# Layer two's unit in a two-layer MLP after attention: seven products in one row, twelve triples in another, its chains queued behind copies, its weights' conversions spread

## The chip, the cores and the metric

The kernel runs on one core of one Trainium2 chip. The metric is the device time of one execution in microseconds; the median of three runs stands for a kernel. One more execution was recorded by the hardware profiler, and all rows below are from that one.

Five engines work side by side, each with its own queue in order: TensorE (PE; its weight loads are listed as PEld), VectorE (DVE), ScalarE (ACT), GpSimd (POOL) and SyncE (SP), which issues the DMAs here. An instruction that has to wait for another engine or a DMA waits at the head of its queue, and all behind it wait too.

## The reference

```python
def _attn_ref(q, k, v):                      # B, H, S, D = 4, 8, 576, 64
    scores = scale * np.matmul(q, k.transpose(0, 1, 3, 2))
    # heads 0-3: mask rel in [0, 32);  heads 4-7: rel >= 0 and same position mod 32
    attn = softmax(np.where(masks, scores, -1e9))
    return np.matmul(attn, v)
x = attn_out.transpose(0, 2, 1, 3).reshape(2304, 512)
# layer one: w_in [512, 2048], w_out [2048, 512]
h = x @ w_in;  g = s * np.maximum(h, 0) ** 2 + b;  x = g @ w_out
# layer two: same shapes
h = x @ w_in;  g = h * np.cos(h);  out = g @ w_out
```

The weights come as 8-byte floats and are converted on the chip. Every operand of a large matmul is split into a high and a low part (two tensors in the matmul's reduced 4-byte format), and each product of matrices is made of three matmuls: high by high, low by high, high by low.

## The kernel before

**Stages.** Attention runs first and overlaps the beginning of layer one. Layer one goes over the 2048 hidden features in four passes (`NPASS`) of 20 slots (`PER`): a slot `t` is one of five blocks of tokens (512 four times, then 256) by one of four groups of 128 features. In a slot `mm_h` makes h in 12 matmuls (4 input chunks, 3 each), `run_act` spreads Relu, Square (ACT), scale and shift (DVE), the high part (ACT) and the low part (DVE) over the ticks that follow, and `mm_2` adds the slot before last into four accumulators in PSUM (12 matmuls). At the end of a block `run_evac` adds the four accumulators to the tile `part` in SBUF: the DVE line L724.

**Background work in layer one.** `bg_step` takes operations of a list that converts the layer's own next weights (`wraw`, `wtmp`); `bg2_step` does the same for layer two's weights, to be stored in DRAM in the form that layer two reads (`wf`, `w2s`). There are 32 such jobs: 16 of `pair_ops` (17 steps each: `praw` loaded, `ta`, `ts`, `ob`, `oa`) and 16 of `out_ops` (9 steps: `oraw`, `tw`, `ow`). The first step of each is an ACT operation (L135) on the raw data that a DMA has landed. `BG2 = 0.85` steps are due after each eighth of a slot from the second pass on; steps left over are done before layer two.

**Layer two** takes three thirds of the tokens (768 each, `SBT`) by eight pairs of feature groups: 24 units `u`. A unit makes h for two groups of 128 features and two halves of 384 tokens by seven products instead of eight (Strassen's scheme with sums shared, on operands that `run_forms` prepares in seven slots of `xhi` and `xlo`). A product is six matmuls of 384 columns into one of two PSUM banks (`pa`, `pb`; they change roles from unit to unit). Copies of a bank to SBUF (`q`, ACT, L1076) and sums of a bank and a copy (`hsum`, DVE, L1049) give the two h of a unit, f = 0 and 1. `run_act2` then makes h·cos(h) of each h: two ACT operations that reduce the argument (`r` L966 and `a` L967), one on DVE (L969), Sin on ACT (L971), the product with h on DVE (L973), high part on ACT and low part on DVE. Six **triples** for each f (three matmuls of 512 columns, `acc`, L1016) add it to six accumulators, which are the output.

**What sets the order.** The code records operations in the order of the list `UNIT`: a product's name, or `t` for one triple. After each entry `beat` advances every generator in `stages` by one step, which places the steps of `run_act2` and `run_forms` between products and triples. A triple is taken from `queue` only if its g was recorded at least `READY_AFTER = 6` beats ago. A scheduler then turns the record into one order for each engine, and moves an operation forward where it reckons the engine idle and the operation ready. `PRODUCTS` gives for each product its weights, its slot of x, its bank, and whether it starts a new sum in the bank or adds to what is there (P6, P7 and P3 add). A product that starts anew, or adds after a copy, may begin only when the copy or sum that reads its bank has ended.

Of the kernel before, what the change touches and what calls it, by code (L numbers as in the profile page):

```python
# [1 line left out]

# [72 lines left out]
    "P1": (0, 0, 0, 0, True),  # L75
    "P5": (1, 0, 1, 1, True),
    "P6": (1, 1, 2, 0, False),
    "P7": (2, 0, 3, 0, False),
    "P2": (0, 1, 5, 0, True),
    "P3": (2, 1, 6, 1, False),  # L80
    "P4": (3, 0, 4, 0, True),
}
LAST_USE = {"P6": 1, "P2": 0, "P3": 2, "P4": 3}
UNIT = ["P1", "t", "P5", "t", "t", "P6", "t", "t", "t", "P7", "t", "t", "t", "P2", "t", "P3", "t", "P4", "t"]
BG2 = 0.85
FORM_PACE = 4
READY_AFTER = 6
LOADS = {
# [9 lines left out]
def net(ctx, tc, qk, rqk, vloc, vstr, rv, w1, w2, s, b, out):  # L98
# [563 lines left out]
    def mm_h(t, c):  # L662
# [4 lines left out]
        for i, (wi, xt) in enumerate(((0, xhi), (0, xlo), (1, xhi))):  # L667
# [7 lines left out]
            )  # L675

    def run_act(t):
# [162 lines left out]
    def run_forms(s_):  # L840
# [30 lines left out]
        whole = (0, HT)  # L871
        yield from split(0, block(0, 0))
        t1 = temp(0)
        sub(t1, b_(0, 1), b_(0, 0), 0, 1)
        yield
        yield from split(1, [(whole, t1)])
        t2 = temp(1)
        sub(t2, b_(1, 1), t_(t1), 1)
        yield
        yield from split(2, [(whole, t2)])  # L880
        t3 = temp(0)
        sub(t3, b_(1, 1), b_(0, 1), 1)
        yield
        yield from split(3, [(whole, t3)])
        sub(t2, b_(1, 0), t_(t2), 0)
        yield
        yield from split(4, [(whole, t2)])
        yield from split(5, block(1, 0))
        yield from split(6, block(1, 1))

    def paced(gen, n):
        for _ in gen:
            for _ in range(n):
                yield

# [18 lines left out]
    for t in range(NSLOT):  # L914
# [35 lines left out]
    while jobs2 or loaded2 or now2[0]:  # L950
# [6 lines left out]
    queue = [("first", t, e) for t in (NSLOT - 2, NSLOT - 1) for e in range(NC)]  # L957
    g2, g2_at = {}, {}
    clock = [0]

    def run_act2(u, f, h, parts):
        gh = gl = None
        for a, b in parts:
# [9 lines left out]
            nc.vector.tensor_tensor(r, h[:, a:b], r, ALU.mult)  # L973
            yield
            if gh is None:
                gh = g_p.tile([P, SBT], F32R, tag="gh", name="gh2")
                gl = g_p.tile([P, SBT], F32R, tag="gl", name="gl2")
            split_hi(gh[:, a:b], r)
# [4 lines left out]
        g2_at[u, f] = clock[0]  # L983

# [9 lines left out]

    def triple(wait=False):

        if not queue:
            return False
        kind, a, *b = queue[0]
        if kind == "first":  # L1000
            queue.pop(0)
            mm_2(a, b[0])
            if b[0] == NC - 1:
                load_w2(4 + a - (NSLOT - 2))
            return True
        f, e = b
        key = a, f
        if key not in g2 or (not wait and clock[0] < g2_at[key] + READY_AFTER):
            return False
        queue.pop(0)  # L1010
        s_, p = divmod(a, NPAIR)
# [15 lines left out]
        if p == NPAIR - 1 and f == 1:  # L1027
            spawn(run_out(s_, e))
        return True

    def beat():
        clock[0] += 1
        tick()

    HALVES = [slice(0, HT), slice(HT, SBT)]
    for u in range(NSB * NPAIR):
        s_, p = divmod(u, NPAIR)
        if p == 0 and s_ + 1 < NSB:
            stages.append(paced(run_forms(s_ + 1), FORM_PACE))
        lastu = u == NSB * NPAIR - 1  # L1040
# [5 lines left out]
        def hsum(f, half, bank, q):  # L1046
            if f not in hs:
                hs[f] = h_p.tile([P, SBT], F32, tag="hs", name="h2")
            nc.vector.tensor_tensor(hs[f][:, HALVES[half]], bank, qs[q], ALU.add)  # L1049

        for what in UNIT:
            if what == "t":
                triple()
                beat()
                continue
            x, fi, j, bi, st = PRODUCTS[what]
            while (s_, j) not in formed:
                beat()
            xh, xl = x_slot(s_, j)
# [7 lines left out]
            if p == NPAIR - 1:  # L1067
                used.add((s_, j))
            if what in LAST_USE:
                i = 4 * u + LAST_USE[what]  # L1070
                del wft[i]
            beat()
            if what in ("P1", "P6", "P7"):
                q = {"P1": 0, "P6": 1, "P7": 2}[what]
                qs[q] = (rem_p, rem_p, gt_p)[q].tile([P, HT], F32, tag=("rq", "rv", "gt")[q], name="q")
                nc.scalar.activation(qs[q], pb[0], AF.Copy)  # L1076
# [10 lines left out]
            if what == "P2":  # L1087
                load_wf(4 * u + 7)
                load_wf(4 * u + 8)
            if what == "P3":  # L1090
                load_wf(4 * u + 9)
            if what == "P4":
                load_wf(4 * u + 10)
        queue.extend(("mm", u, f, e) for f in range(2) for e in range(SBT // P))
    while queue:
        triple(True)
        beat()
    while stages:
# [74 lines left out]
```

## Time and profile before

| | us |
|---|---|
| median of three runs | 884.03 |
| the three runs | 884.03, 890.0, 883.83 |
| the profiled execution | 889.94 |
| its span, first to last instruction | 888.2 |
| PE busy in the span | 869.2 |
| DVE busy | 594.4 |
| ACT busy | 515.2 |

The profiled execution is like the slowest of the three runs, 5.9 above the median. A busy PE is not one at its pace: a matmul's end is modelled, and the pace is read from one start to the next.

### The profile page before, as it was taken

The numbers are of one execution on the slowest core, as the hardware profiler recorded it, in microseconds if no ns is written. First come the engines' busy times: TensorE is split into PE (matmuls) and PEld (weight loads), VectorE is DVE, ScalarE is ACT, GpSimd is POOL, SyncE is SP. The second block draws the span as 40 slices with busy tenths as digits, with TensorE's granted clock in tenths as the row PEclk, the third lists the DMA queues.
The fourth block names the chain that finished last, engine by engine and source line by source line (L and its number), as shares of the span: only waits on it lengthen the run. The fifth ranks groups of instructions, "written<-read, shape, count | busy, mean of one in ns | idle before, by whom it ended". The sixth has DMA issues, their size and how long they took to land.

```text
span 888.2 us, 13475 instructions
## 1 busy us (share of the span) xinstructions
PE 869.2 (98%) x4901; PEld 737.8 (83%) x4901; DVE 594.4 (67%) x1265; ACT 515.2 (58%) x1123; POOL 4.0 (0%) x15
## 2 busy tenths in 40 slices
PE   8899999999999999999999989999999999999998
PEld 5577777898777887888888978989889898988986
DVE  5978889999889996343579564547745446554554
ACT  5878898667556654343466363646646355463544
POOL 1000000000000000000000000000000000000000
PEclk9989999999999999999999999999999999999999
DMA  9655442775667662012104555655665565755611
GB/s 271 186 148 163 146 144 76 270 261 175 221 249 247 222 212 74 1 48 72 47 10 180 195 174 176 202 168 187 216 212 201 167 194 180 246 198 166 205 56 72
DMA packets 65058, 147.39 MB, mean 166 GB/s; under 512 B 6256, under 2 KB 24688, under 8 KB 64992
## 3 DMA queue, kind: packets, MB, share of 16 engines
q1 hardware_dynamic: 64992, 146.53, 50.2%
q8 instruction: 39, 0.64, 0.3%
q14 instruction: 27, 0.22, 0.1%
HBM read 118.72 MB, written 27.79 MB: 165 GB/s over the span
## 4 chain that ended last, share of the span: by engine, by line
PE 76%; DVE 10%; DMA 7%; ACT 4%; issue 2%; SPq 1%; ACTq 0%; DVEq 0%
PE acc L1016 22%; PE h_ps L668 14%; PE acc L704 14%; PE pa L1064 10%; PE pb L1064 10%; DMA wraw<-in_w_dram 3%; PE o_ps L533 3%; PE s_ps L500 2%; PE t_ps L457 1%; DMA wearly<-in_w_dram 1%; DVE part L724 1%; ACT part L432 1%; DVE r L687 1%; DVE gl L130 1%; DMA praw<-in_w_dram 1%
## 5 line engine op out<-in xcount | busy, mean ns | idle before, releaser
L704 PE MATMUL acc<-gh,w 128*128 128x512 f32 (+1 forms) x640 | 198.0, 371 | 5.1 <-DVE part L724 5.0
L668 PE MATMUL h_ps<-xhi,w 128*128 128x512 f32 (+1 forms) x640 | 197.9, 372 | 1.0 <-ACT w L127 1.0
L1016 PE MATMUL acc<-w2l,gh 128*128 128x512 f32 x576 | 180.1, 393 | 0.0
L704 PEld LDWEIGHTS acc<-gh,w 128*128 128x128 f32 x640 | 117.3, 188 | 27.9 <-DVE part L724 8.1
L668 PEld LDWEIGHTS h_ps<-xhi,w 128*128 128x128 f32 x640 | 117.0, 189 | 22.0 <-ACT w L127 1.2
L668 PE MATMUL h_ps<-xlo,w 128*128 128x512 f32 (+1 forms) x320 | 119.3, 373 | 0.1
L704 PE MATMUL acc<-gl,w 128*128 128x512 f32 (+1 forms) x320 | 118.3, 370 | 0.0
L1016 PEld LDWEIGHTS acc<-w2l,gh 128*128 128x128 f32 x576 | 106.8, 189 | 11.9
L1016 PE MATMUL acc<-w2l,gl 128*128 128x512 f32 x288 | 114.2, 397 | 0.0
L966 ACT ACTIVATE r<-h 128x768 f32<-128x768 f32 (+1 forms) x50 | 41.0, 820 | 114.5 <-DVE h L1049 114.2
L127 ACT ACTIVATE gh<-r 128x512 fp32r<-128x512 f32 (+3 forms) x130 | 87.5, 675 | 34.3 <-DVE r L687 28.0
L130 DVE TENSOR_TENSOR gl<-r,gh 128x512 fp32r<-128x512 f32 (+3 forms) x130 | 96.6, 745 | 14.6 <-ACT gh L127 13.5
L1064 PE MATMUL pb<-xhi,wfl 128*128 128x384 f32 x336 | 100.7, 340 | 2.4 <-ACT q L1076 2.4
L1064 PE MATMUL pa<-xhi,wfl 128*128 128x384 f32 x336 | 99.9, 338 | 0.0
L681 ACT ACTIVATE r<-h_ps 128x512 f32<-128x512 f32 (+1 forms) x80 | 43.9, 549 | 64.0 <-PE h_ps L668 63.9
L1049 DVE TENSOR_TENSOR h<-pb,q 128x384 f32<-128x384 f32 x48 | 26.7, 557 | 74.2 <-PE pb L1064 48.5
L1049 DVE TENSOR_TENSOR h<-pa,q 128x384 f32<-128x384 f32 x48 | 26.7, 557 | 69.2 <-PE pa L1064 48.6
L668 PEld LDWEIGHTS h_ps<-xlo,w 128*128 128x128 f32 x320 | 60.5, 189 | 10.6 <-DVE xlo L130 0.4
L704 PEld LDWEIGHTS acc<-gl,w 128*128 128x128 f32 x320 | 60.3, 189 | 9.7
L1064 PEld LDWEIGHTS pb<-xhi,wfl 128*128 128x128 f32 x336 | 62.6, 189 | 6.6 <-ACT q L1076 3.0
L1064 PEld LDWEIGHTS pa<-xhi,wfl 128*128 128x128 f32 x336 | 62.2, 188 | 3.6
L687 DVE TENSOR_SCALAR r<-r,sb 128x512 f32<-128x512 f32 (+1 forms) x72 | 37.0, 513 | 42.0 <-ACT r L682 41.8
(105 smaller groups left out, 1280.0 us busy)
## 6 DMA issues: line engine op xcount, KB each, us to landing
wfl<-wf SPq DMA_DIRECT2D x72, 512.0 KB, 4.6
w2l<-w2s SPq DMA_DIRECT2D x48, 512.0 KB, 3.3
wraw<-in_w_dram SPq DMA_DIRECT2D x56, 256.0 KB, 3.2
praw<-in_w_dram SPq DMA_DIRECT2D x32, 256.0 KB, 3.4
oraw<-in_w_dram SPq DMA_DIRECT2D x16, 512.0 KB
wf<-ob SPq DMA_DIRECT2D x16, 512.0 KB, 2.7
w2s<-ow SPq DMA_DIRECT2D x16, 512.0 KB, 4.3
wfl<-wf SPq DMA_DIRECT2D x24, 256.0 KB, 2.7
```

The source lines that it names most:

```text
L127: nc.scalar.activation(dst_hi, src, AF.Copy)
L130: nc.vector.tensor_tensor(dst_lo, src, hi.bitcast(F32), ALU.subtract)
L500: it.last = nc.tensor.matmul(it.s_ps[po : po + lq.shape[1], co : co + lk.shape[1]], lq, lk, start=not pe_mask, stop=True, skip_group_check ...
L533: nc.tensor.matmul(dst, vs, pt, start=True, stop=True)
L668: nc.tensor.matmul(h_ps[t][:, :tb], wt[:, wi, c * P : (c + 1) * P], xt[:, c, t0 : t0 + tb], start=(c == 0 and i == 0), stop=(c == NC - 1 a ...
L681: nc.scalar.activation(r, h, AF.Relu)
L687: nc.vector.tensor_scalar(r, r, sb[:, 0:1], sb[:, 1:2], ALU.mult, ALU.add)
L704: nc.tensor.matmul(o, wt[:, wi, e * P : (e + 1) * P], g, start=f == 0 and i == 0, stop=f == FP - 1 and i == 2, skip_group_check=True,)
L966: nc.scalar.activation(r, h[:, a:b], AF.Copy, bias=0.25, scale=INV_2PI)
L1016: nc.tensor.matmul(accs[e], g[:, e * P : (e + 1) * P], w[:, wi, :], start=p == 0 and f == 0 and i == 0, stop=p == NPAIR - 1 and f == 1 and ...
L1049: nc.vector.tensor_tensor(hs[f][:, HALVES[half]], bank, qs[q], ALU.add)
L1064: nc.tensor.matmul(pb[bi], a, b[:, m, :], start=st and m == 0 and i == 0, stop=m == 1 and i == 2, skip_group_check=True)
```

## The change

The seven products of a unit now stand in one row and its twelve triples in another. `UNIT` is `P1 P2 P6 P5 P7`, then one `t` that stands for all twelve triples, then `P3 P4`, which the next unit's `P1` follows. The triples are those of the unit before last (`TRIPLE_LAG = 2`), with no clock of beats; in units 0 and 1 four accumulations left from layer one stand in their place (`first`), and 24 triples follow after the last unit.

P2 changes banks and sums with the copy of P1 while P6 is made. The steps of f = 0 are recorded from P3 on as before. Those of f = 1 now start only after P5 of the **next** unit, and are tied: `r` is issued behind the copy of P6 of that unit, `a` behind the copy of P7. `tc.issue_after(x)` gives no wait at run time; it holds an operation behind `x` in the order of the engine that both run on. `run_forms` moves one step after every four triples, behind the last copy and the last sum, and prepares the slots in another order.

In layer one the pace of the conversions of layer two's weights is 0.85 in the second and third pass and 1.25 in the fourth, and the first step of each job is tied behind the last Relu that was recorded. A Sin on one element is recorded in slot 64, behind a Relu, so that the ACT table with Sin is loaded there.

```diff
 PRODUCTS = {
     "P1": (0, 0, 0, 0, True),
-    "P5": (1, 0, 1, 1, True),
+    "P2": (0, 1, 1, 1, True),
     "P6": (1, 1, 2, 0, False),
...
-UNIT = ["P1", "t", "P5", "t", "t", "P6", "t", "t", "t", "P7", "t", "t", "t", "P2", "t", "P3", "t", "P4", "t"]
-BG2 = 0.85
+UNIT = ["P1", "P2", "P6", "P5", "P7", "t", "P3", "P4"]
+BG2 = (0.0, 0.85, 0.85, 1.25)
 FORM_PACE = 4
-READY_AFTER = 6
+TRIPLES = 12
+TRIPLE_LAG = 2
...
                 now2[0] = loaded2.pop(0)
                 bg2_load()
+                with tc.issue_after(relu[0].ins):
+                    next(now2[0])()
+                continue
...
-        nc.scalar.activation(r, h, AF.Relu)
+        relu[0] = nc.scalar.activation(r, h, AF.Relu)
...
+        if last == 4:
+            with tc.issue_after(relu[0].ins):
+                nc.scalar.activation(sb[:, 4:5], sb[:, 3:4], AF.Sin)
...
-                bg2_step(BG2)
+                bg2_step(BG2[t // PER])
...
+        def act(step, *args, **kw):
+            key = (after or {}).get(step)
+            with tc.issue_after(evac[key].ins) if key else nullcontext():
+                nc.scalar.activation(*args, **kw)
...
-            nc.scalar.activation(r, h[:, a:b], AF.Copy, bias=0.25, scale=INV_2PI)
-            nc.scalar.activation(m, r, AF.Copy, bias=MAGIC)
+            act("r", r, h[:, a:b], AF.Copy, bias=0.25, scale=INV_2PI)
+            while held("m"):
+                yield
+            act("m", m, r, AF.Copy, bias=MAGIC)
...
+    def form_step(u):
+        if forms and (u, 2) in evac:
+            with tc.issue_after(evac[u, 2].ins), tc.issue_after(added[u].ins):
+                if next(forms[0], "end") == "end":
+                    forms.pop(0)
+
+    def triples(u):
+        n = 0
+        while queue and (n < NC if queue[0][0] == "first" else queue[0][1] <= u - TRIPLE_LAG):
+            triple()
+            tick()
+            n += 1
+            if n % FORM_PACE == 0:
+                form_step(u)
+        for _ in range(n, TRIPLES):
+            tick()
...
+            if what == "P2":
+                hsum(0, 0, pb[1], 0)
+            if what == "P5" and u:
+                spawn(run_act2(u - 1, 1, h1.pop(), [(0, SBT)], {"r": (u, 1), "m": (u, 2)}))
             if what == "P7":
                 hsum(1, 1, pb[1], 2)
-            if what == "P2":
-                hsum(0, 0, pb[0], 0)
             if what == "P3":
                 hsum(0, 1, pb[1], 1)
                 spawn(run_act2(u, 0, hs[0], parts))
             if what == "P4":
                 hsum(1, 0, pb[0], 2)
-                spawn(run_act2(u, 1, hs[1], parts))
+                if lastu:
+                    spawn(run_act2(u, 1, hs[1], parts))
+                else:
+                    h1.append(hs[1])
```

**PE in a unit of layer two.** Before, products (`pa`, `pb`; five rows, six matmuls) and triples (`acc`; two rows) change places all along the unit:

```order
L1016 MATMUL acc_5419<-w2l,gl_6432 128x512
L1064 MATMUL pa<-xhi,wfl 128x384
L1064 MATMUL pa<-xlo,wfl 128x384
L1064 MATMUL pa<-xhi,wfl 128x384 x2
L1064 MATMUL pa<-xlo,wfl 128x384
L1064 MATMUL pa<-xhi,wfl 128x384
L1016 MATMUL acc_5420<-w2l,gh_6431 128x512 x2
L1016 MATMUL acc_5420<-w2l,gl_6432 128x512
L1016 MATMUL acc_5421<-w2l,gh_6431 128x512 x2
L1016 MATMUL acc_5421<-w2l,gl_6432 128x512
L1064 MATMUL pb<-xhi,wfl 128x384
```

Of the changed kernel, the end of a row of twelve triples and the first two products, P3 and P4, of the row of seven:

```order
L1028 MATMUL acc_5425<-w2l,gh_6579 128x512 x2
L1028 MATMUL acc_5425<-w2l,gl_6580 128x512
L1090 MATMUL pb<-xhi,wfl 128x384
L1090 MATMUL pb<-xlo,wfl 128x384
L1090 MATMUL pb<-xhi,wfl 128x384 x2
L1090 MATMUL pb<-xlo,wfl 128x384
L1090 MATMUL pb<-xhi,wfl 128x384
L1090 MATMUL pa<-xhi,wfl 128x384
L1090 MATMUL pa<-xlo,wfl 128x384
L1090 MATMUL pa<-xhi,wfl 128x384 x2
```

Seven products follow one another with no triple between them, and so do twelve triples.

**ACT in a unit of layer two.** Before, in one unit of the last third (`r` and `a` reduce the argument, the second `r<-r` line is Sin, `gh` the high part, `q` a copy):

```order
L1076 ACTIVATE q<-pb 128x384 x2
L966 ACTIVATE r_7155<-h_7139 128x768
L967 ACTIVATE a_7156<-r_7155 128x768
L966 ACTIVATE r_7173<-h_7122 128x768
L967 ACTIVATE a_7174<-r_7173 128x768
L971 ACTIVATE r_7155<-r_7155 128x768
L1076 ACTIVATE q<-pa 128x384
L971 ACTIVATE r_7173<-r_7173 128x768
L127 ACTIVATE gh_7192<-r_7155 128x768
L127 ACTIVATE gh_7209<-r_7173 128x768
L1076 ACTIVATE q<-pa 128x384 x2
```

Of the changed kernel, from f = 0 of one unit (`r_6891`) to its f = 1 (`r_6945`):

```order
L973 ACTIVATE r_6891<-h_6796 128x768
L973 ACTIVATE a_6892<-r_6891 128x768
L1099 ACTIVATE q<-pa 128x384
L988 ACTIVATE r_6891<-r_6891 128x768
L1099 ACTIVATE q<-pa 128x384
L973 ACTIVATE r_6945<-h_6831 128x768
L973 ACTIVATE gh_6933<-r_6891 128x768
L1099 ACTIVATE q<-pa 128x384
L973 ACTIVATE a_6946<-r_6945 128x768
L988 ACTIVATE r_6945<-r_6945 128x768
L129 ACTIVATE xhi<-part 128x2x384
L973 ACTIVATE gh_6981<-r_6945 128x768
```

The three copies of the next unit (P1, P6, P7) now stand one by one in the chain of f = 0, each behind one or two operations on 768 columns, and f = 1 follows them.

**ACT in layer one.** Before, a stretch of the second pass (Relu L681, Square L682, first steps of jobs `ta` and `tw`):

```order
L681 ACTIVATE r<-h_ps 128x512
L682 ACTIVATE r<-r 128x512
L135 ACTIVATE tw<-oraw 128x512
L127 ACTIVATE gh<-r 128x512
L127 ACTIVATE ob<-ts 128x4x128
L127 ACTIVATE oa<-ta 128x2x128
L127 ACTIVATE oa<-ta 128x128
L135 ACTIVATE tw<-oraw 128x512
L681 ACTIVATE r<-h_ps 128x512
```

Of the changed kernel, also in the second pass:

```order
L688 ACTIVATE r<-h_ps 128x512
L137 ACTIVATE tw<-oraw 128x512
L689 ACTIVATE r<-r 128x512
L129 ACTIVATE w_3673<-wtmp 128x512
L129 ACTIVATE gh<-r 128x512
L137 ACTIVATE wtmp<-wraw 128x256
L129 ACTIVATE ow<-tw 128x512
L137 ACTIVATE wtmp<-wraw 128x256
L688 ACTIVATE r<-h_ps 128x512
```

A job's first step now stands right behind a Relu and ahead of that slot's Square. Counted over the whole order of ACT, the 32 first steps stood 10, 16, 1 and 5 to the four passes, and stand 1, 9, 11 and 11 now.

## Rows read from the trace of the kernel before

**Rows 1.** Windows: stretch, length, busy us of PE, PEld, DVE, ACT, POOL, clock, DMA share.
```profile
206.00:304.00 98.00, 93.55 (x445) 77.41 (x444) 88.56 (x206) 60.20 (x121) 0.00 (x0) 1.00 0.67 227
304.00:402.00 98.00, 97.31 (x470) 81.68 (x469) 60.01 (x135) 45.52 (x90) 0.00 (x0) 1.00 0.30 94
499.00:884.00 385.00, 382.63 (x1896) 343.84 (x1895) 207.27 (x279) 200.69 (x295) 0.00 (x0) 1.00 0.54 179
```
**Rows 2.** Waits: who waited for whom, us in total, times, longest.
```profile
PE acc L704 <- DVE part L724: 5.0, 7, 1.6
```
**Rows 3.** Timeline, 229 to 233 us, ACT, DVE and PE: start, us, instruction [idle before].
```profile
229.92 0.43 ACT L135 ACTIVATE wtmp<-wraw 128x256 f32<-128x256 f32 x1 [2.97 <-DMA wraw<-in_w_dram]
...
230.91 0.55 DVE L687 TENSOR_SCALAR r<-r,sb 128x512 f32<-128x512 f32 x1 [2.92 <-ACT r L682]
...
230.12 0.39 PE L704 MATMUL acc<-gh,w 128*128 128x512 f32 x1
232.11 0.50 PE L704 MATMUL acc<-gh,w 128*128 128x512 f32 x1 [1.60 <-DVE part L724]
```
**Rows 4.** Windows of the tile praw alone: stretch, length, busy DVE, ACT (counts), clock, DMA.
```profile
206.00:304.00 98.00, 9.63 (x14) 5.23 (x8) 1.00 0.67 227
```
**Rows 5.** The chain that ended last, one unit of layer two: start, us, matmuls.
```profile
622.73 1.39 PE acc L1016 x6
...
627.24 1.06 PE pa L1064 x6
...
638.49 1.39 PE acc L1016 x6
```
**Rows 6.** Timeline, PE, 508 to 510 us: two products in succession.
```profile
508.13 0.33 PE L1064 MATMUL pa<-xhi,wfl 128*128 128x384 f32 x1
508.30 0.33 PE L1064 MATMUL pa<-xlo,wfl 128*128 128x384 f32 x1
...
509.17 0.33 PE L1064 MATMUL pb<-xhi,wfl 128*128 128x384 f32 x1
```
**Rows 7.** Timeline, PE, 871 to 875 us: first, fourth and fifth of the last triples.
```profile
871.31 0.63 PE L1016 MATMUL acc<-w2l,gh 128*128 128x512 f32 x2
...
873.39 0.62 PE L1016 MATMUL acc<-w2l,gh 128*128 128x512 f32 x2
...
874.07 0.62 PE L1016 MATMUL acc<-w2l,gh 128*128 128x512 f32 x2
```
**Rows 8.** Timeline, 648 to 652 us: a product's successor on PE, its sum, the chain's start.
```profile
648.82 0.63 PE L1016 MATMUL acc<-w2l,gh 128*128 128x512 f32 x2
649.02 0.56 DVE L1049 TENSOR_TENSOR h<-pa,q 128x384 f32<-128x384 f32 x1 [1.20 <-PE pa L1064]
649.67 0.85 ACT L966 ACTIVATE r<-h 128x768 f32<-128x768 f32 x1 [5.07 <-DVE h L1049]
650.55 0.85 ACT L967 ACTIVATE a<-r 128x768 f32<-128x768 f32 x1
651.37 0.85 ACT L966 ACTIVATE r<-h 128x768 f32<-128x768 f32 x1
```
**Rows 9.** Timeline, 511 to 516 us, ACT and PE: the beginning of layer two.
```profile
511.31 0.47 ACT L1076 ACTIVATE q<-pb 128x384 f32<-128x384 f32 x1
511.80 1.28 ACT L971 ACT_TABLE_LOAD   x1
...
511.83 0.44 PE L1064 MATMUL pb<-xhi,wfl 128*128 128x384 f32 x1 [0.42 <-ACT q L1076]
512.11 0.34 PE L1064 MATMUL pb<-xlo,wfl 128*128 128x384 f32 x1
...
515.10 0.52 PE L1064 MATMUL pb<-xhi,wfl 128*128 128x384 f32 x1 [1.95 <-ACT q L1076]
```
**Rows 10.** Windows: the two stretches at the lower clock, columns as in rows 1.
```profile
44.30:51.10 6.80, 6.80 (x54) 5.69 (x54) 4.80 (x14) 3.73 (x8) 0.00 (x0) 0.50 0.40 117
...
515.30:518.70 3.40, 3.40 (x10) 3.04 (x10) 3.01 (x5) 2.64 (x4) 0.00 (x0) 0.50 0.03 11
```

More of the change, by code (lines that the diff above doesn't have):

```diff
@@ L1 @@
 import math
+from contextlib import nullcontext
 import concourse.bass as bass
@@ L75 @@
     "P1": (0, 0, 0, 0, True),
-    "P5": (1, 0, 1, 1, True),
+    "P2": (0, 1, 1, 1, True),
     "P6": (1, 1, 2, 0, False),
-    "P7": (2, 0, 3, 0, False),
-    "P2": (0, 1, 5, 0, True),
+    "P5": (1, 0, 3, 1, True),
+    "P7": (2, 0, 4, 0, False),
     "P3": (2, 1, 6, 1, False),
-    "P4": (3, 0, 4, 0, True),
+    "P4": (3, 0, 5, 0, True),
 }
-LAST_USE = {"P6": 1, "P2": 0, "P3": 2, "P4": 3}
-UNIT = ["P1", "t", "P5", "t", "t", "P6", "t", "t", "t", "P7", "t", "t", "t", "P2", "t", "P3", "t", "P4", "t"]
-BG2 = 0.85
+LAST_USE = {"P2": 0, "P5": 1, "P3": 2, "P4": 3}
+UNIT = ["P1", "P2", "P6", "P5", "P7", "t", "P3", "P4"]
+BG2 = (0.0, 0.85, 0.85, 1.25)
 FORM_PACE = 4
-READY_AFTER = 6
+TRIPLES = 12
+TRIPLE_LAG = 2
 LOADS = {
@@ L675, in mm_h @@
             )
+    relu = [None]
     def run_act(t):
@@ L872, in run_forms @@
         yield from split(0, block(0, 0))
+        yield from split(1, block(1, 0))
         t1 = temp(0)
@@ L875, in run_forms @@
         yield
-        yield from split(1, [(whole, t1)])
         t2 = temp(1)
@@ L880, in run_forms @@
         yield from split(2, [(whole, t2)])
+        yield from split(3, [(whole, t1)])
         t3 = temp(0)
@@ L883, in run_forms @@
         yield
-        yield from split(3, [(whole, t3)])
+        yield from split(4, [(whole, t3)])
         sub(t2, b_(1, 0), t_(t2), 0)
         yield
-        yield from split(4, [(whole, t2)])
-        yield from split(5, block(1, 0))
+        yield from split(5, [(whole, t2)])
         yield from split(6, block(1, 1))
[L891 to L894, printed above, removed]
     wft, w2t = {}, {}
@@ L957, in net, with run_act2, held @@
     queue = [("first", t, e) for t in (NSLOT - 2, NSLOT - 1) for e in range(NC)]
-    g2, g2_at = {}, {}
-    clock = [0]
-    def run_act2(u, f, h, parts):
+    g2 = {}
+    evac, added = {}, {}
+    def run_act2(u, f, h, parts, after=None):
         gh = gl = None
+        def act(step, *args, **kw):
+            key = (after or {}).get(step)
+            with tc.issue_after(evac[key].ins) if key else nullcontext():
+                nc.scalar.activation(*args, **kw)
+        def held(step):
+            return after and step in after and after[step] not in evac
         for a, b in parts:
@@ L974, in run_act2 @@
             yield
+            while held("hi"):
+                yield
             if gh is None:
@@ L977, in run_act2 @@
                 gl = g_p.tile([P, SBT], F32R, tag="gl", name="gl2")
-            split_hi(gh[:, a:b], r)
+            act("hi", gh[:, a:b], r, AF.Copy)
             yield
@@ L982, in run_act2 @@
         g2[u, f] = (gh, gl)
-        g2_at[u, f] = clock[0]
     def run_out(s_, e):
@@ L993, in run_out, with triple @@
         nc.sync.dma_start(out=out[r0 : r0 + P, :], in_=o)
[L995 to L999, printed above, removed]
+    def triple():
+        kind, a, *b = queue.pop(0)
         if kind == "first":
-            queue.pop(0)
             mm_2(a, b[0])
@@ L1004, in triple @@
                 load_w2(4 + a - (NSLOT - 2))
-            return True
+            return
         f, e = b
         key = a, f
-        if key not in g2 or (not wait and clock[0] < g2_at[key] + READY_AFTER):
-            return False
-        queue.pop(0)
         s_, p = divmod(a, NPAIR)
@@ L1028, in triple @@
             spawn(run_out(s_, e))
[L1029 to L1033, printed above, removed]
+    forms = []
+    def form_step(u):
[13 more added lines that the diff above has]
+            tick()
     HALVES = [slice(0, HT), slice(HT, SBT)]
+    h1 = []
     for u in range(NSB * NPAIR):
@@ L1038, in net @@
         if p == 0 and s_ + 1 < NSB:
-            stages.append(paced(run_forms(s_ + 1), FORM_PACE))
+            forms.append(run_forms(s_ + 1))
         lastu = u == NSB * NPAIR - 1
@@ L1048, in hsum @@
                 hs[f] = h_p.tile([P, SBT], F32, tag="hs", name="h2")
-            nc.vector.tensor_tensor(hs[f][:, HALVES[half]], bank, qs[q], ALU.add)
+            added[u] = nc.vector.tensor_tensor(hs[f][:, HALVES[half]], bank, qs[q], ALU.add)
         for what in UNIT:
             if what == "t":
-                triple()
-                beat()
+                triples(u)
                 continue
@@ L1057, in net @@
             while (s_, j) not in formed:
-                beat()
+                tick()
             xh, xl = x_slot(s_, j)
@@ L1068, in net @@
                 used.add((s_, j))
[L1069 to L1072, printed above, removed]
+            tick()
             if what in ("P1", "P6", "P7"):
@@ L1085, in net @@
                 hsum(1, 0, pb[0], 2)
-                spawn(run_act2(u, 1, hs[1], parts))
[L1087 to L1093, printed above, removed]
+                if lastu:
+                    spawn(run_act2(u, 1, hs[1], parts))
+                else:
+                    h1.append(hs[1])
+            if what in LAST_USE:
+                x = LAST_USE[what]
+                del wft[4 * u + x]
+                load_wf(4 * u + 7 + x)
         queue.extend(("mm", u, f, e) for f in range(2) for e in range(SBT // P))
-    while queue:
-        triple(True)
-        beat()
+    triples(NSB * NPAIR - 1 + TRIPLE_LAG - 1)
+    triples(NSB * NPAIR - 1 + TRIPLE_LAG)
     while stages:
```

2 lines of the change are left out of this document (1 added, 1 removed).

## The prediction

> **What bounds the kernel now.** I read the busy time by stages first [rows 1]. From 499 us on, layer two, PE is busy 382.6 of 385 us, so only two things can shorten it there: a better pace, or the 2.4 us without work. In the second pass of layer one PE is busy 93.6 of 98 us, in the third 97.3: 5.1 us idle, at DVE loads of 88.6 and 60.0. The waits say for whom [rows 2]: seven times an accumulator that DVE's additions (L724) had not yet emptied, 5.0 us. One of them followed backward [rows 3]: a layer-one weight (`wraw`) lands late, ACT stands 2.97 us before its first step, the Square queued behind it is late, DVE waits 2.92 us for the Square with the additions queued behind, and PE starts its next matmul at 232.11, 1.99 us after the last one, where the pace is 0.23. That is 0.16 more than the idle time of 1.60 that the row names, since a modelled end lies behind the next start.
>
> Then the pace. One unit of layer two takes 638.49 - 622.73 = 15.76 us [rows 5]. A product in it takes 1.06 us, a triple 1.39 / 2 = 0.70. At the beginning of layer two products follow one another, 508.13 to 509.17: 1.04 [rows 6]. After the last product the triples follow one another; the first takes 0.70, three take 873.39 - 871.31 = 2.08, and from there each takes 874.07 - 873.39 = 0.68 [rows 7]. So changing from 384 to 512 columns costs about 2.08 - 3 x 0.68 = 0.04 us, changing back about 0.02 (1.06 against 1.04), and a unit that changes as often as before never reaches its pace.
>
> Last, the beginning of layer two [rows 9]: PE stands twice, before 511.83 and before 515.10, for copies that ACT makes late, since the loading of a table, 1.28 us, and operations of 0.85 stand ahead of them. From 515.3 to 518.7 the granted clock is 0.50, the lower level of 1.2 GHz, after PE had started nothing for over 2 us [rows 10].
>
> **The change part by part.**
>
> *The two rows.* Work on PE stays: 168 products, 288 triples. One unit at the undisturbed pace is 7 x 1.04 + 12 x 0.68 = 15.44; with one change each way 15.44 + 0.06 = 15.50. Against 15.76 that is 0.26 a unit. 22 of the 24 units have the pattern before (the last triples already stand in a row, the first units have few triples): 22 x 0.26 = **5.7 us less**. If only the 0.02 of a product went and triples stayed at 0.70 it would be 22 x 0.14 = 3.1; if changes cost nothing at all, 22 x 0.32 = 7.0.
>
> *The rule against it.* The rows say that the pace depends on what ran before. The Trainium skill, "TensorE: Matmul & The Clock Gate", section "Back-to-back issue gap", has no such term: a warm matmul starts its columns / 2.4 GHz plus 2.5 ns after the one before, whatever that was. An estimate by that page is 42 x 162.5 + 36 x 215.8 ns = 14.6 us a unit in either order, and the rows would save nothing. The trace disagrees with it in both ways, with 15.76 a unit and a pace that settles after three triples [rows 5, 7].
>
> *Copies in the row.* What the triples between products covered is now uncovered: P6 of the next unit adds to the bank of P1, so P1's copy must end while P2 is made. In the new order of ACT, `r` and `a` of f = 0 stand ahead of that copy. Count from the end of P3, whose sum starts that chain [rows 8]: sum starts 649.02 - 648.82 = 0.20 later, takes 0.56, `r` starts at 0.85 (649.67), `a` at 1.73 (650.55), the next operation at 2.55 (651.37), here the copy, 0.47 long, and PE starts 0.05 after a copy (511.31 + 0.47 = 511.78, then 511.83) [rows 9]: 3.07 us. P4, P1 and P2 take 3.12. It fits by 0.05 us. When the wait ends late, the matmul after it also starts late: 0.28 to the next start in place of 0.17 [rows 6, 9], 0.11 more. P5 waits for P2's sum, which stands on DVE behind one operation of f = 0 (0.95 us) that starts when `a` ends, 2.6 + 0.9 + 0.56 + 0.05 = 4.1 against 4.16: as close. P7's copy stands behind one Sin, and has 0.3 us to spare. I take **1.0 us more** in 22 units, between 0 and 22 x 0.11 = 2.4.
>
> *f = 1 a unit later.* Its steps end about 13 us after P3's sum, within 15.5, and its triples come a unit later, so nothing waits for them. Two more g's are alive; the pool has three, and the fourth is needed only when six triples are done. Nothing. The slots of `run_forms` are needed a third later. Nothing, with the triples as cover.
>
> *The beginning of layer two.* The table is loaded in slot 64, under PE's work, and no second load stands in the order of ACT. Before, the two stands cost 0.42 and 1.95 us idle, each with 0.27 more (0.16 as above, 0.33 - 0.17 here, and the 0.11), and 3.4 us at half the clock cost 1.7: 4.6. After, unit 0's products come in one row at once and only 12 matmuls of 256 columns cover its chains. I follow the new order: the sum of P7 in unit 1 stands behind unit 0's low part, and P3 waits some 0.4 us; the sum after P3 stands behind unit 0's f = 1 and four additions of layer one, some 13.5 us after unit 0's P3, but five triples of unit 0 stand there on PE ahead of the next product, so that hardly 0.3 remain. **3.9 us less**, between 4.6 less and 2 more (if those triples have to wait for the additions as well).
>
> *Conversions.* In the second pass 16 first steps stood, eight of them on `praw` [rows 4], and one in the third; now it is 9, then 11 and 11. A job costs DVE about (9.63 / 8 for `praw`'s steps alone) two to four us, so the second pass gets some 20 us lighter and the third some 30 heavier, about 70 to 80 of 98 in each. The seven waits cost 5.0 + 7 x 0.27 = 6.9 us. Those that came of jobs whose loads and stores ran into one another should go, since a load is now issued a whole job ahead (7 us or more). Those that came of `wraw`, as the one followed above, have no reason to go, and the third pass, with one job, had 0.7 us of them. I take **3.0 us less**, between all 6.9 and 1 more: a first step stands right ahead of a Square now, where a late load stops just the chain that stopped PE at 230 us. The first step on ACT costs the same 0.67 us wherever it stands, off PE's path. The faster pace in the fourth pass has PE's full 97 us to hide in.
>
> **Sum.** 5.7 - 1.0 + 3.9 + 3.0 = 11.6 us. The profiled execution took 889.94; 889.94 - 11.6 = 878.3. It is 5.9 above the median, and the trace can't show what the runs at 884 lack. If it lies in attention, which the change leaves alone, the median falls by the same 11.6 to 872.4. If the runs at 884 simply had fewer of the 11.5 us of stalls that I take away, they fall to 878 too. For the first speaks a stretch of 6.8 us at the lower clock in attention [rows 10], longer than the one at 515; nothing shows that other runs lack it, so this is a choice: **872.4 us**.
>
> **The rivals.**
>
> (1) *Layer one keeps its stalls.* They move from jobs to `wraw` and into the third pass, 6.9 us in all. For it: PE lost 0.7 us in the third pass, which had one job [rows 1]. Against: DVE's load falls where most were. 872.4 + 3.0 = 875.4.
>
> (2) *The order costs nothing.* The slower pace within a unit comes of something else than the changes of length, such as the addresses of the operands, and stays in rows. For it: the six accumulators' triples at the end differ from others in nothing but their row, and only one such row was seen; against: that row, and the products at 508 us. The 5.7 are lost and the close copies with them: 884.03 - 3.9 - 3.0 = 877.1. This is the rule of the Trainium skill's page above, in what it says of order.
>
> (3) *The runs at 884 lacked the stalls already*: 878.3, as worked out.
>
> (4) *The row waits for its copies: slower.* If something delays `r` or `a` of f = 0 (an addition of run_out, a form's operation, a Sin not yet done) by one operation of 0.85 us, P6 starts 0.8 late, with 0.11 more, and P5 behind it: 22 x 0.9 = 20 us, 892.4. It gets slower than before once the delay exceeds (884.0 - 872.4) / 22 = 0.53 us a unit. For it: the fit is 0.05 us. Against: ACT and DVE have 13 us of chain in 15.5 and stand idle before P3.
>
> **How the numbers follow.** Chances: forecast 0.52; (1) 0.17; (2) 0.08; (3) 0.14; (4) 0.06; others 0.03. The range: low, all stalls and 7.0 of the rows, 884.0 - 7.0 - 4.6 - 6.9 = 865.5, and (4) with part of its delay and the ends of (2) and (3) up to 882; this leaves out (4) and a few more. 1%, 8.8 us, is about what this kernel's runs tell from no change; faster by more means under 875.2. The forecast's own spread (868 to 877) lies mostly under it, (1) half: 0.46 + 0.09 = 0.55. (4) and half of the others are slower: 0.06. The rest, 0.39, is within 1%.
>
> **What would show it.** In the changed kernel's profile: a unit of 15.5 to 15.6 us; twelve triples in 8.2, seven products in 7.3; P6 and P5 start without idle time, or the wait names `q` or the sum; no wait of over 1 us before 530 us in layer two and no lower clock there; L724 named in at most half of 5 us of waits, and those after a `wraw`. I am wrong if the unit stays at 15.7 with no idle time (2), if P6 stands at each unit (4), or if passes two to four show 5 us idle again (1).

## The result and the profile after

The changed kernel takes 875.0 us (873.69 to 877.59, 4 runs), the kernel before 885.08 beside it (883.83 to 890.0, 4 runs): a ratio of 0.9877, 95% interval 0.9845 to 0.9909. It is faster by 1.2%, 10 us. The forecast was 872.4, with a range of 865.5 to 882.0.

The profiled execution of the changed kernel took 877.59 us, its span is 875.8. The two spans can be cut at three matmuls that PE's timeline shows in each kernel: the first of the second pass of layer one, the first of layer two's products, and the last one of the last triple. The times between them (us):

| | start to pass two | passes two to four | layer two | last matmul to end |
|---|---|---|---|---|
| before | 195.44 | 303.41 | 385.20 | 4.11 |
| changed | 199.05 | 295.98 | 375.85 | 4.93 |
| gain | -3.61 | 7.43 | 9.35 | -0.82 |

So the two stages that the change touches give back 16.8 us, and the start took 3.6 more in this execution, in which PE stood 4.13 us before a matmul of attention at 22.14 us, with the lower clock (0.50) from 21.7 to 28.5. The windows of these stages, of the changed kernel (columns as in [rows 1]: three passes, then layer two):

```profile
199.05:297.70 98.65, 98.65 (x482) 83.59 (x481) 80.47 (x187) 56.50 (x117) 0.00 (x0) 1.00 0.48 164
297.70:396.40 98.70, 98.70 (x483) 83.62 (x482) 82.38 (x187) 56.62 (x115) 0.00 (x0) 1.00 0.54 181
396.40:495.03 98.63, 98.63 (x482) 83.57 (x481) 76.61 (x158) 56.55 (x106) 0.00 (x0) 1.00 0.49 174
495.03:870.88 375.85, 375.85 (x1897) 339.00 (x1896) 212.36 (x290) 202.60 (x298) 0.00 (x0) 1.00 0.55 183
```

PE is busy all of 671.8 us, at the full clock. The waits of PE over the whole span, its longest three:

```profile
PE o_ps L538 <- issue: 4.1, 1, 4.1
PE dummy L764 <- DVE part L760: 1.2, 1, 1.2
PE t_ps L462 <- DVE sm L451: 1.1, 1, 1.1
```

All three lie ahead of the second pass; from there to the end no wait of PE is listed. The line of [rows 2], an accumulator that waits for the additions to `part` (now L731), is not in the list at all. The unit, by the chain that ended last:

```profile
572.89 1.06 PE pa L1090 x6
573.95 1.04 PE pb L1090 x6
...
579.18 1.04 PE pa L1090 x6
580.23 8.20 PE acc L1028 x36
588.43 1.06 PE pb L1090 x6
```

From one P3 to the next it takes 588.43 - 572.89 = 15.54 us, where [rows 5] have 15.76: seven products 7.34, twelve triples 8.20. The close copies, in the timeline of the same unit (P4's first matmul, the sum of P3 that starts the chain, `r`, `a`, P1's copy, P2's last matmul, P6's first):

```profile
573.79 0.33 PE L1090 MATMUL pb<-xhi,wfl 128*128 128x384 f32 x1
...
573.99 0.56 DVE L1076 TENSOR_TENSOR h<-pa,q 128x384 f32<-128x384 f32 x1 [2.78 <-PE pa L1090]
...
574.64 0.85 ACT L973 ACTIVATE r<-h 128x768 f32<-128x768 f32 x1 [4.42 <-DVE h L1076]
...
575.52 0.85 ACT L973 ACTIVATE a<-r 128x768 f32<-128x768 f32 x1
...
576.27 0.47 ACT L1099 ACTIVATE q<-pa 128x384 f32<-128x384 f32 x1
...
576.74 0.34 PE L1090 MATMUL pb<-xhi,wfl 128*128 128x384 f32 x1
576.92 0.34 PE L1090 MATMUL pa<-xhi,wfl 128*128 128x384 f32 x1
```

The copy ends at 576.74, P6 starts at 576.92, 0.18 later, where 0.05 is enough [rows 9]: 0.13 us to spare. P6 carries no idle time, and neither does P5.

### The profile page after: what moved, and what is told of

Read it like the earlier page. It is cut to its first block, busy times and chain, and to the rows that moved or that the text cites. A ratio compares the mean times of both kernels' runs of the same rounds, so it can differ in the third digit from the quotient of the medians.

```text
span 875.8 us, 13488 instructions
## 1 busy us (share of the span) xinstructions
PE 861.7 (98%) x4901; PEld 735.0 (84%) x4901; DVE 596.0 (68%) x1265; ACT 513.0 (59%) x1124; POOL 4.0 (0%) x15
## 4 chain that ended last, share of the span: by engine, by line
PE 96%; ACT 2%; DVE 1%; issue 1%; DMA 0%; ACTq 0%; DVEq 0%
PE h_ps L673 23%; PE acc L711 22%; PE acc L1028 22%; PE pa L1090 10%; PE pb L1090 10%; PE o_ps L538 3%; PE s_ps L505 2%; PE t_ps L462 2%; ACT part L437 1%; PE dummy L764 0%; PE s_ps L500 0%; DVE sm L422 0%; PE dummy L519 0%; DMA out_dram<-o 0%; ACT part L470 0%
## 5 line engine op out<-in xcount | busy, mean ns | idle before, releaser
L711 PE MATMUL acc<-gh,w 128*128 128x512 f32 (+1 forms) x640 | 195.6, 370 | 0.0
L129 ACT ACTIVATE gh<-r 128x512 fp32r<-128x512 f32 (+1 forms) x80 | 46.9, 586 | 40.5 <-DVE r L694 40.2
L1028 PEld LDWEIGHTS acc<-w2l,gl 128*128 128x128 f32 x288 | 54.0, 188 | 11.2
L986 DVE SCALAR_TENSOR_TENSOR r<-a,r 128x768 f32<-128x768 f32 (+1 forms) x50 | 46.2, 926 | 21.7 <-ACT a L973 21.7
L988 ACT ACTIVATE r<-r 128x768 f32<-128x768 f32 (+1 forms) x50 | 40.8, 820 | 32.1 <-DVE r L986 32.1
```

Source lines behind the costliest of these rows:

```text
L129: nc.scalar.activation(dst_hi, src, AF.Copy)
L711: nc.tensor.matmul(o, wt[:, wi, e * P : (e + 1) * P], g, start=f == 0 and i == 0, stop=f == FP - 1 and i == 2, skip_group_check=True,)
L986: nc.vector.scalar_tensor_tensor(r, m, MAGIC, r, ALU.subtract, ALU.subtract)
L988: nc.scalar.activation(r, r, AF.Sin, scale=-TWO_PI)
L1028: nc.tensor.matmul(accs[e], g[:, e * P : (e + 1) * P], w[:, wi, :], start=p == 0 and f == 0 and i == 0, stop=p == NPAIR - 1 and f == 1 and ...
```

## The experiments

**First pair: which half of the change gives what.** Rows only is the changed kernel without the tie of a job's first step, with the old pace, and without the early Sin:

```diff
-BG2 = (0.0, 0.85, 0.85, 1.25)
+BG2 = (0.0, 0.85, 0.85, 0.85)
...
-                with tc.issue_after(relu[0].ins):
-                    next(now2[0])()
-                continue
...
-        if last == 4:
-            with tc.issue_after(relu[0].ins):
-                nc.scalar.activation(sb[:, 4:5], sb[:, 3:4], AF.Sin)
```

Expected: 

> The changed unit of layer two alone: the pace of the conversions stays at 0.85 to the end, their first steps are not tied, the table is loaded when layer two needs it. My account: layer one (second pass to the first product) keeps its stalls, 303 us as before; layer two's unit takes 15.5 in place of 15.76; from the first to the last of layer two 378 to 380 in place of 385.2, since the table still loads there. Time 5 to 7 us below before. Rival (the runs at 884 lack layer one's stalls, the rows are all of the gain): 9 to 10 us below before.

Conversions only is the kernel before with just those three things added, and its unit as it was. Expected: 

> The conversions and the early table alone, with the unit of layer two as before. My account: layer one 296 in place of 303.4 us, unit 15.76, layer two 383 to 385 (the table's 1.28 gone). Time 7 to 9 us below before, so that this and the unit alone add to more than the whole change's 10 us. Rival (the runs at 884 lack layer one's stalls): 1 to 4 us below before, though the profile may show more.

One execution each of the kernel before and of the changed kernel went with them, profiled, to see which stages repeat. Expected of the first: 

> The kernel before, profiled once more. My account (the stalls belong to the kernel): layer one 303 us with L724 named in about 5 us of waits, and two stands at the beginning of layer two. Rival (they come and go with how DMAs land, and the first profile was of a run with many): an execution near 884 to 886 with layer one at 297 to 300, or without the stretch at the lower clock at 515 us.

And of the second: 

> The changed kernel, profiled once more. In the first profile PE stood 4.1 us in attention with nothing named, about 18 us from the start (2.1 us before the change, named ACT). If that is chance, as I hold since the order of the engines up to there is the same, it is absent or another length here and the span is 871 to 873; rival (the change causes it): again about 4 us, span 875 to 876. Layer one 296 and layer two 376 in either case.

Measured (ratio to the kernel before on the same chip, with its 95% interval; stages in us, cut as above):

| | time | ratio | start to pass two | passes two to four | layer two |
|---|---|---|---|---|---|
| rows only | 879.87 | 0.9891 (0.9869 to 0.9913) | 192.46 | 302.92 | 376.36 |
| conversions only | 879.43 | 0.9878 (0.986 to 0.9896) | 195.68 | 295.98 | 382.28 |
| before, again | 886.01, one run | | 192.75 | 303.35 | 383.69 |
| changed, again | 871.66, one run | | 192.76 | 295.98 | 376.13 |

Each half alone brings its own stage, and the conversions also 2.9 us of layer two. Passes two to four take 303 us with the old conversions and 296 with the new ones, whatever the unit. Layer two takes 376 with the new unit. The stages repeat to 0.3 us in the changed kernel, and to 1.5 in the one before; what changes from execution to execution is the start (192 to 199). The changed kernel's start was 199.05 and is 192.76 now, 0.01 from the kernel before; PE's stand of 4.1 us in attention is not there, so the changed kernel does not always have it; that the change has no part in it is not shown. By their times alone, rows only (10.2 us less) would fit its rival and conversions only (10.6 less) saved more than expected; it is the stages that decide, and they speak against the rival, since the execution at 886.01 has all of layer one's stalls and conversions only has none. Both halves take away stands at the beginning of layer two, which is one reason why they add to more than the whole. The waits of PE with rows only keep the line that the changed kernel lost:

```profile
PE acc L708 <- DVE part L728: 4.8, 5, 1.4
```

With conversions only the beginning of layer two still has both stands of [rows 9], the second at 0.58 idle in place of 1.95:

```profile
504.64 0.44 PE L1072 MATMUL pb<-xhi,wfl 128*128 128x384 f32 x1 [0.42 <-ACT q L1084]
...
506.54 0.44 PE L1072 MATMUL pb<-xhi,wfl 128*128 128x384 f32 x1 [0.58 <-ACT q L1084]
```

No table is loaded there now. So in the old unit the early table took 1.4 us from the second stand and left the first.

**The tie alone.** The changed kernel without the tie; the new pace and the early Sin stay:

```diff
-                with tc.issue_after(relu[0].ins):
-                    next(now2[0])()
-                continue
```

Expected: 

> The changed kernel without the tie of a job's first step behind a Relu; the new pace (0.85, 0.85, 1.25) stays, and so do the rows and the early Sin. Counted over ACT's order the 32 first steps stand 10, 16, 4 and 2 to the four passes again, in place of 1, 9, 11 and 11. Theory: the tie spread the conversions and ended layer one's stalls. Then layer one (first matmul of the second pass to the first product of layer two) takes about 303 us again, in place of 296.0, with some 5 us of waits behind the additions to part; layer two stays at 376; in all some 7 us more than the changed kernel. Rival: the pace did it, or the early table load, and layer one stays at 296.

It takes 881.59 us (874.76 to 884.81, 10 runs), ratio 0.9907 (0.9882 to 0.9931). Passes two to four take 304.26, layer two 376.32. The waits of PE have the old line again:

```profile
PE acc L708 <- DVE part L728: 4.9, 4, 3.3
```

The window of the second pass, its first matmul to the third pass's first:

```profile
195.49:302.43 106.94, 101.96 (x482) 84.54 (x481) 95.54 (x224) 65.84 (x134) 0.00 (x0) 0.98 0.69 226
```

The pace without the tie is worth nothing; the stalls are back, and at the same place. The longest ends at 234 us, again behind a `wraw` that ACT waits for:

```profile
231.97 0.43 ACT L137 ACTIVATE wtmp<-wraw 128x256 f32<-128x256 f32 x1 [3.17 <-DMA wraw<-in_w_dram]
```

One of the ten executions took 874.76 us, no longer than with the tie. It was not the profiled one, so whether it had the stalls is not known.

**The table alone.** The changed kernel without the early Sin:

```diff
-        if last == 4:
-            with tc.issue_after(relu[0].ins):
-                nc.scalar.activation(sb[:, 4:5], sb[:, 3:4], AF.Sin)
```

Expected: 

> The changed kernel without the early Sin, so that the table with Sin is loaded in layer two's first chain again. Theory: with the new rows twelve triples or matmuls of 256 columns lie between the first chain and the products that wait for copies, so the load's 1.28 us are covered: layer two stays at 375.9 to 376.4 us and the time within 1 us of the changed kernel's. Rival: the early load was worth what the prediction gave to it, and without it PE stands at the beginning of layer two again, 1.3 (the load alone) to 4.6 us more, 377 to 380.5 us of layer two.

875.19 us (874.01 to 876.06), ratio 0.9843 (0.9818 to 0.9869), on the same chip as the run without the tie. Layer two takes 375.84, 0.01 from the changed kernel. The table is loaded in layer two's first chain again, by the timeline of ACT:

```profile
502.04 1.28 ACT L985 ACT_TABLE_LOAD   x1
```

PE does not stand there, by the window from layer two's first product to the first product of its fourth unit:

```profile
491.43:524.56 33.13, 33.13 (x189) 31.44 (x187) 20.63 (x35) 20.39 (x32) 0.00 (x0) 1.00 0.70 229
```

The early load is worth nothing once the products stand in a row; in the old order the second stand was 1.4 us shorter with it.

**How close the copies are.** ACT's second step of f = 0 is done again on 384 columns, ahead of P1's copy:

```diff
+            if f == 0 and len(parts) == 1:
+                again[u] = nc.scalar.activation(m[:, :HT], r[:, :HT], AF.Copy, bias=MAGIC)
...
-                evac[u, q] = nc.scalar.activation(qs[q], pb[0], AF.Copy)
+                with tc.issue_after(again[u - 1].ins) if what == "P1" and u else nullcontext():
+                    evac[u, q] = nc.scalar.activation(qs[q], pb[0], AF.Copy)
```

Expected: 

> The changed kernel with one operation more on ACT in each of 23 units: the second step of f = 0 is done again on 384 of its columns, ahead of the copy of P1, so that this copy comes some 0.37 to 0.45 us later. Theory, by the prediction's count of the chain (3.07 against 3.12 us): P6 starts 0.3 to 0.4 us late in each unit with 0.11 more behind the wait, a unit takes about 16.0 us in place of 15.54, layer two some 10 us more (386). Rival: the count left something out and there is slack in the chain; a unit stays under 15.6 and the time within 2 us of the changed kernel's.

880.76 us (879.19 to 881.3), ratio 0.9904 (0.9879 to 0.9929). Layer two takes 383.00, 7.2 us more than in the changed kernel, where 10 were expected. The chain of one unit runs over ACT now (P3 at 569.33, P3 of the next unit at 585.22: 15.89 us):

```profile
569.33 1.08 PE pa L1092 x6
...
572.85 0.53 ACT a L986
573.37 0.39 ACT q L1102
573.76 0.04 issue
573.80 1.33 PE pa L1092 x6
...
585.22 1.08 PE pb L1092 x6
```

The timeline of PE in the same unit:

```profile
573.36 0.40 PE L1030 MATMUL acc<-w2l,gh 128*128 128x512 f32 x1
573.80 0.45 PE L1092 MATMUL pa<-xhi,wfl 128*128 128x384 f32 x1
574.09 0.34 PE L1092 MATMUL pa<-xlo,wfl 128*128 128x384 f32 x1
```

The added operation takes 0.53 with its step of 0.02. The scheduler put one matmul of a triple (0.23 us from start to start) between P2 and P6, as a filler into the wait it foresaw. P6 starts 573.80 - 573.36 = 0.44 after it, 0.21 late, and its second matmul 0.29 after its first in place of 0.17. The account closes: the copy comes 0.55 later; less the 0.13 to spare and the 0.23 filled, that is 0.19. With 0.11 behind the wait and 0.03 for the change of length around the filler it is 0.33, and the unit is 0.35 longer. So the prediction's count (0.05 to spare) was right to 0.08 us, the copies do stand on the edge, and what was expected of this run was too much by the filler.

**The order alone.** One triple each between products, the rest in the row (the lines that read the new entries are left out):

```diff
-UNIT = ["P1", "P2", "P6", "P5", "P7", "t", "P3", "P4"]
+UNIT = ["P1", "1", "P2", "1", "P6", "1", "P5", "1", "P7", "t", "P3", "1", "P4", "1"]
```

Expected: 

> The changed kernel with five of the twelve triples of a unit put one by one between products (P1 1 P2 1 P6 1 P5 1 P7, seven triples, P3 1 P4 1, so six places where triples stand, one of them with seven or six); everything else as before, the same lag. Theory: a change of column count costs about 0.06 us there and back, so five more changes cost 0.25 to 0.35 a unit and the unit takes about 15.8, layer two some 5 to 6 us more. Rival: order costs nothing by itself and the old unit's slower pace came of its waits or its operands; the unit stays at 15.54.

A unit has only twelve triples, so four stand singly and eight in the row, and the two last places stay empty: five changes there and back, where the changed kernel has one and the kernel before seven. The chain of one unit:

```profile
569.06 1.06 PE pa L1097 x6
570.13 1.04 PE pb L1097 x6
571.17 1.04 PE pa L1097 x6
572.21 0.70 PE acc L1028 x3
572.91 1.06 PE pb L1097 x6
573.97 0.70 PE acc L1028 x3
...
579.25 5.48 PE acc L1028 x24
584.73 1.06 PE pb L1097 x6
```

The unit takes 584.73 - 569.06 = 15.67 us: a product after a triple takes 1.06, one after a product 1.04; a single triple 0.70, one in the row 5.48 / 8 = 0.685. One, five and seven changes there and back give 15.54, 15.67 and 15.76, which is 0.13 / 4 = 0.03 and 0.22 / 6 = 0.04 us for one. The order does cost, by about half of what was expected of this run. Layer two takes 378.60, 2.75 more. In the time, 875.77 (874.56 to 876.18; ratio 0.9849, 0.9824 to 0.9873), that does not stand out; it is the unit that tells.

**Place or load?** The tie did two things at once: it put a first step behind a Relu, and it left fewer jobs to the second pass (9 in place of 16). Two kernels take them apart by the pace alone. Tied, with 16 jobs in the second pass:

```diff
-BG2 = (0.0, 0.85, 0.85, 1.25)
+BG2 = (0.0, 1.35, 0.85, 0.85)
```

Expected: 

> The changed kernel with the tie, but a pace of 1.35, 0.85 and 0.85, so that the second pass has 16 first steps again, as before the change (counted over ACT's order 1, 16, 10 and 5). Theory: the stalls of the second pass came of its load, 16 jobs beside the layer's own conversions, on DVE and on the DMA queues, and the tie helped by sending fewer there. Then DMA's share in the second pass is about 0.67 again, the waits for additions come back there (4 to 6 us), and layer one takes 300 to 302 us. Rival: a first step behind a Relu, in the order in which its data land, is what ended the stalls, and layer one stays at 296 with 16 jobs too.

Not tied (the edit of the tie alone, above), with `BG2 = (0.0, 0.1, 0.85, 1.25)`. Expected: 

> The changed kernel without the tie, and with a pace of 0.1 in the second pass, so that 11 first steps stand there (10, 11, 0 and 11 in the four passes), two more than in the changed kernel. Theory that the load made the stalls: with five jobs less in the second pass most of its 5 to 8 us go, and layer one takes 296 to 298 us. Rival, that the place of the first step behind a Relu ended them: the stalls stay without the tie, layer one takes 300 us or more, and the wait near 230 us for the additions is there again.

Tied with sixteen takes 875.06 us (873.41 to 876.25), ratio 0.9838 (0.9806 to 0.987), and passes two to four 295.96. Its second pass:

```profile
196.02:294.66 98.64, 98.64 (x482) 83.56 (x481) 93.97 (x222) 63.72 (x133) 0.00 (x0) 1.00 0.70 234
```

The second pass of the kernel before, cut at the same matmuls:

```profile
195.44:300.26 104.82, 100.37 (x482) 83.37 (x481) 94.60 (x222) 65.37 (x134) 0.00 (x0) 1.00 0.67 224
```

DVE has the same work within 1% and the DMA queues within 2% (share times length), and the pass takes 6.2 us less. So the load alone does not make the stalls. What differs is what ACT waits for. Of the kernel before, from 195 to 295 us, ACT's waits for DMAs:

```profile
ACT wtmp L135 <- DMA wraw<-in_w_dram: 5.9, 6, 3.0
...
ACT ob L127 <- DMA wf<-ob: 3.6, 1, 3.6
ACT tw L135 <- DMA oraw<-in_w_dram: 3.1, 2, 2.2
ACT ta L135 <- DMA praw<-in_w_dram: 2.9, 3, 1.4
```

And of the tied kernel with sixteen:

```profile
ACT wtmp L137 <- DMA wraw<-in_w_dram: 2.1, 4, 1.2
ACT ow L129 <- DMA wf<-ob: 1.4, 2, 0.9
...
ACT ta L137 <- DMA praw<-in_w_dram: 0.3, 1, 0.3
```

In the changed kernel only `wraw` is left of these four:

```profile
ACT wtmp L137 <- DMA wraw<-in_w_dram: 3.8, 5, 1.3
```

All twelve profiles go the same way: in passes two to four the seven with the tie show no wait of PE, and the five without it show two to seven behind the additions.

Not tied with eleven jobs, passes two to four take 298.69, and its second pass is stalled still, at a DMA share and a DVE load below the kernel before:

```profile
196.86:298.23 101.37, 99.57 (x482) 83.34 (x481) 88.84 (x208) 62.12 (x129) 0.00 (x0) 1.00 0.62 207
```

Half of what both theories said holds: a lighter pass stalls less (2.7 us in place of 6.2 over 98.64) and still stalls. The wait near 230 us is gone, those near 254 and 277 us stay; but the one near 230 varies by itself (1.60 and 0.84 us in the two profiles of the kernel before). Its time says nothing on layer one (889.53, 885.51 to 892.28; ratio 0.9993, 0.9972 to 1.0014): jobs are left over into layer two, where PE stands for a sum behind them (timeline of PE), and layer two takes 388.30:

```profile
507.71 0.44 PE L1087 MATMUL pb<-xhi,wfl 128*128 128x384 f32 x1 [1.11 <-DVE h L1073]
...
512.99 0.69 PE L1087 MATMUL pb<-xhi,wfl 128*128 128x384 f32 x1 [3.97 <-DVE h L1073]
```

## Why the prediction came out, step by step

The total was right within its range, and the sign and the size of the gain too. By its own steps:

**The two rows, and the copies in the row.** The prediction took 5.7 less and 1.0 more, 4.7 net; measured 22 x (15.76 - 15.54) = 4.8. The net is right, the parts are not: the copies cost nothing, and the rows bring 0.22 a unit in place of 0.26, since a product in the row takes 1.04 to 1.07 and not 1.04 (seven 7.34, counted 7.28 and 0.02). The two errors cancel, which is luck. That P6 would fit by a hair is shown: 0.13 us to spare, and with the copy 0.55 later the unit pays.

**The rule against it** fell. The kernel with single triples has the same matmuls, no wait in the unit, and a time of the unit that goes with the number of changes. The Trainium skill, "TensorE: Matmul & The Clock Gate", section "Back-to-back issue gap", gives spacings by columns alone, the one that the prediction used for an isolated matmul and another for a sustained stream; the three units disagree with both (15.54, 15.67 and 15.76 for the same matmuls). Rival (2) goes with it.

**f = 1 a unit later**: nothing, as taken; PE waits for no g.

**The beginning of layer two.** Taken 3.9 less, by difference 385.20 - 375.85 - 4.8 = 4.55, as much as the two stands and the lower clock (4.6); the two waits that were counted against it (0.4 and 0.3) don't show. But the first reason given, the table under PE's work, is not the cause: with the table late, layer two takes the same 375.84. The rows did it, and the early table had its worth only in the old order. What the stretch at the lower clock cost is no sure gain: the kernel before, profiled again, had the same two stands without it, and layer two took 1.5 us less.

**Conversions: the term that failed in size.** Taken 3.0 less, measured 7.4, above the term's own bound of 6.9. The step that failed is "Those that came of `wraw`, as the one followed above, have no reason to go", and with it the reading that the second pass stalls for its load ("some 20 us lighter"; DVE's busy time fell by 14, from 94.60 to 80.47). In the third pass "some 30 heavier" on 60 would be 90 and not "70 to 80"; it is 82.38. All stalls went, those behind a `wraw` too, and with sixteen jobs in the pass they stay away. Tied behind a Relu, a job's first step finds its data landed: with sixteen jobs ACT waits for `praw` and `oraw` 0.3 us in place of 6.0, and for `wraw` 2.1 in place of 5.9. That the tie ends the stalls is shown; by which of these waits is not. ACT still waits 3.8 us for `wraw` in the changed kernel, in waits of at most 1.3 us, and PE stands for none of them. How the `wraw` loads gain from the place of the others' steps was not tried by itself: SP issues all of them in one order, and which neighbour it is stays open. Rival (1) fell: the third pass, with 11 jobs and DVE at 82.4, has no stall.

**The starting point: a choice that was half right.** From the profiled execution the forecast was 889.94 - 11.6 = 878.3; the changed kernel's profiled execution came at 877.59. But that nearness is luck and holds two errors: the stages gave 16.8, and the start took 3.6 longer, the end 0.8 (the last sums' copies wait for a store of `out`, not followed further). The median of 884.03 was low beside later ones: 37 runs of the kernel before on three chips lie from 885.9 to 892.8, with medians of 889 to 890. Against those, kernels that equal the changed one in both stages, the late table and the tied sixteen, save 14 us (0.9843 and 0.9838), near the 16.0 of the stages with the end. So a term that was 4.4 too small stood on a start that was some 5 too low, and the two errors work against each other: with 889.3 for a start the same sum gives 877.7, as far above the 875.0 measured as 872.4 is below. What the two runs at 884 lacked is not recorded. The profile of the execution at 886.01 may show the kind: 2.7 us less ahead of the second pass, where the stretch at the lower clock took 3.4 us in place of 6.8 [rows 10] (half of the difference, 1.7 us, is an estimate of what that saves), no lower clock in layer two, and all of layer one's stalls. Rival (3), that they lacked the stalls, has 1.5 us for it; the choice, that it lies in attention, at most 2.7.

**Rival (4)** did not come, but its mechanism is real: 0.55 us on ACT ahead of one copy brings back 7.2 of the 9.35 us that layer two had gained.

## What to carry to other kernels

Where a matrix engine never waits, cut the number of changes of shape in its stream: each costs little (here 0.03 to 0.04 us there and back), but there were six to spare in each of 22 units; count then, copy by copy, whether what had covered the neighbours' chains is still there. Work from another stage that is slipped into an engine's queue should stand where its data have landed: as many jobs in the same pass stalled the kernel or did not, by the place of their first steps. And take a starting point from more than three runs where the profiled one stands aside from them.

## What the runs showed of the chip

After a stand of PE of about 2 us the granted clock fell to the lower level of 1.2 GHz in one execution and not in another. In the kernel before it did at 515 us [rows 10]; in its second profile the stand of 1.95 us came too and the clock stayed (window right behind it):

```profile
512.30:515.70 3.40, 3.36 (x16) 2.90 (x17) 3.03 (x4) 2.73 (x4) 0.00 (x0) 1.00 0.17 58
```

In the changed kernel without the tie, after the longest stand of 3.3 us in layer one, it fell:

```profile
235.40:238.80 3.40, 3.40 (x9) 2.64 (x8) 3.40 (x9) 1.84 (x5) 0.00 (x0) 0.50 0.23 54
```

Not tied with eleven jobs, it fell while PE stood the 3.97 us that end at 512.99 us, and for twice as long:

```profile
510.80:517.60 6.80, 4.62 (x14) 4.62 (x15) 2.96 (x6) 2.11 (x3) 0.00 (x0) 0.50 0.90 291
```

So in these runs a stand cost its length, 0.11 us behind it, and in some executions the stretch at half the clock: 1.7 us more for one of 3.4 us with PE busy throughout.
